# One change in three places of an attention and mixture-of-experts kernel: softmax scalings with an accumulator output, the second expert's rows transposed on TensorE, the last routing round's products placed later

## The chip, the cores and the metric

The kernel runs on one core of one Trainium2 chip. Its engines are TensorE (PE, with its weight loads counted apart as PEld), VectorE (DVE), ScalarE (ACT), GpSimd (POOL) and SyncE (SP), which here only issues DMAs. Each engine works through its own list of instructions in the order in which the program wrote them. The metric is the time of one execution on the device in microseconds, taken as the median of several runs.

## What is computed

Causal attention by blocks of 64 over 8 batches, 8 heads, 576 positions and a head size of 64; its output, as 4608 tokens of 512 numbers, goes through 8 experts. Each token is given to one expert, greedily by the largest logits, and each expert takes 576 tokens.

```python
scores = scale * np.matmul(q, k.transpose(0, 1, 3, 2))
scores = np.where(mask, scores, -1000000000.0)
scores = scores - np.max(scores, axis=-1, keepdims=True)
attn = np.exp(scores)
attn = attn / (np.sum(attn, axis=-1, keepdims=True) + 1e-09)
x = np.matmul(attn, v)          # then to (4608, 512)
logits = x @ w_gate             # (4608, 8)
for idx in np.argsort(-logits.flatten()):
    tok, e = idx // 8, idx % 8
    if assigned[tok] >= 0 or counts[e] >= 576: continue
    assigned[tok] = e; counts[e] += 1
for e in range(8):
    h = np.maximum(x[assigned == e] @ w1[e], 0.0)
    out[assigned == e] = h @ w2[e]
```

## The kernel before

**A planner writes the order.** All work is written as generators that yield steps such as `yield D, 70, events`: the engine (D is DVE, A is ACT, T is TensorE, G is POOL, S is SP), a planned cost in ns, and the planned events that the step needs. `Sched.run` (line 113) keeps a clock for each engine and always takes the step that could start first, with priorities for near ties. The order in which steps are taken is the order of the instructions on each engine. Planned costs and events set only that order; at run time an engine waits on semaphores for the data that an instruction really needs. A step that names two engines, 'AD' or 'GD', goes to the one whose planned end is earlier, with a bias.

**Attention** works on 32 pairs of heads (`n`), each as 128 partitions that hold a 64-row block of two heads. `scores` (line 330) multiplies with TensorE in three groups of row blocks, `GROUPS`; two score buffers exist in PSUM. `softmax` (line 355) runs once for each pair and group, 96 times: DVE takes row maxima (line 366), scales them by minus the softmax factor (line 369, two to four numbers per partition), ACT takes the exponential with these as bias and sums the rows (line 373), DVE adds 1e-9 to the sums (line 385) and takes the reciprocal (line 387), and POOL (line 395), in one case DVE (line 393), multiplies the probabilities. `transpose` (line 405) turns them with TensorE (line 421), and ACT (line 401) or DVE (line 403) copies them out of PSUM; the planner chooses. `values` (line 426) multiplies with v, `rows` writes x to DRAM, `logits` makes the logits. The small numbers of a pair stand in a tile `m` of [128, 4, 9]: row 0 maxima, row 1 scaled maxima, row 2 sums, row 3 reciprocals. DVE also makes a shifted copy of k (line 327) and residuals of q and k (line 277, DVE or POOL).

**Experts.** `route(k)` (line 653) finds in 14 search steps (lines 712 to 737: counts on DVE and ACT, a small TensorE product `tot`) the expert that fills up next and its threshold. It then numbers its tokens with the TensorE products `po` (lines 794 to 801) and DVE steps (803 to 814), updates the logits in `out` (lines 817 to 824, with `full`, lines 784 to 788) and so starts route k+1. `invert` (line 828) turns the numbers into a list of row indices: comparisons OH and OL and products RH on DVE (lines 832 to 839), TensorE products `pe` (line 846) and `ps` (line 853), the list `ix` at line 856. For k = 0 one of the RH products is ACT's (line 833) and `out` comes after the RH step, as `s.late`. The last round, k = 7, has no search.

`gather` (line 910) fetches the expert's rows with five indirect DMAs from POOL's queue. `flip` (line 923) brings them into column form: for k = 0 with eight TensorE transposes for each block of 128 rows (line 928) and a copy by ACT and one by DVE (lines 932, 933), for the others with a DMA transpose from SP's queue (line 942). `weights` (line 865) loads an expert's weights in eight pieces of 512 KB from SP's queue; ACT and POOL (for the first pieces of experts 0 and 1 ACT and DVE) split them into two half-precision parts (lines 876 to 889). The second four pieces of expert 1 wait in the plan for the event 'fl',1, that its rows have been flipped.

`ffn(k)` (line 945) makes h (line 967, in two halves of tokens), its halves HH and HL (lines 953, 955), then y for five blocks of rows (lines 992, 996). `yev` copies y out (line 975, for the last block also line 979) and scatters it to the output with an indirect DMA from POOL's queue (line 983); three output buffers `y` exist.

The lines that set the places spoken of:

```python
yield D,440 if k==0 else 800                       # 837
yield T,350,'rt'                                   # 841: before the pe products
yield G,1038,('ffn',k-2),('xm',k-1,m)              # 915: before a gather
yield G,1038,('yo',s.ny-1)                         # 982: before a scatter
```

## Time and profile before

| | |
|---|---|
| median of 3 runs | 846.4 us (844.75 to 847.79) |
| the profiled execution | 841.47 us, its span 839.7 us |
| granted TensorE clock, mean | 0.948 |
| PE busy | 736.4 us (88%) |
| DVE busy | 628.2 us (75%) |
| ACT busy | 533.3 us (64%) |
| POOL busy | 458.2 us (55%) |
| DMA traffic | 126.77 MB, 151 GB/s on average |

The profile is one execution, recorded by the hardware profiler. A group's row gives the line of the program, engine, operation, tiles (out<-in), shapes and count; behind the first bar the busy us of the group and the mean ns of one; behind the second the idle time of the engine just before them and what ended it. A row of the view of one line gives minimum, median and maximum ns. A row of the timeline gives the start in us, the duration in us and, in brackets, how long the engine had been idle and what released it. The chain of waits is followed back from the last instruction, at each step to what released it.

Attention ends at about 372 us. A routing round with TensorE mostly idle follows to about 412 us, then the eight experts to about 825 us, then the last scatters.

### The profile page before, as it was taken

The numbers are of one execution on the slowest core, as the hardware profiler recorded it, in microseconds if no ns is written. First come the engines' busy times: TensorE is split into PE (matmuls) and PEld (weight loads), VectorE is DVE, ScalarE is ACT, GpSimd is POOL, SyncE is SP. The second block draws the span as 40 slices with busy tenths as digits, with TensorE's granted clock in tenths as the row PEclk, the third lists the DMA queues.
The fourth block names the chain that finished last, engine by engine and source line by source line (L and its number), as shares of the span: only waits on it lengthen the run. The fifth ranks groups of instructions, "written<-read, shape, count | busy, mean of one in ns | idle before, by whom it ended". The sixth has DMA issues, their size and how long they took to land.

```text
span 839.7 us, 18356 instructions
## 1 busy us (share of the span) xinstructions
PE 736.4 (88%) x6253; PEld 460.4 (55%) x6253; DVE 628.2 (75%) x2300; ACT 533.3 (64%) x1443; POOL 458.2 (55%) x497
## 2 busy tenths in 40 slices
PE   5888998888898889971599699999999997999995
PEld 3555555555565566650454474756647464475752
DVE  7999999899989999748798796977778697020210
ACT  5777876677787777824483487777684947373210
POOL 5787776677776777610240346647390835665101
PEclk9999998899999999985699899999999999999998
DMA  9799998899879989732613718375563919763101
GB/s 193 146 184 165 189 182 160 161 185 203 188 143 175 180 162 200 171 77 57 214 45 121 201 51 269 103 247 118 206 150 118 232 45 277 220 137 76 33 13 44
DMA packets 291757, 126.77 MB, mean 151 GB/s; under 512 B 256336, under 2 KB 274768, under 8 KB 291664
## 3 DMA queue, kind: packets, MB, share of 16 engines
q1 hardware_dynamic: 285776, 106.73, 58.0%
q0 software_dynamic: 5888, 18.88, 7.4%
q8 instruction: 49, 0.80, 0.4%
q14 instruction: 44, 0.36, 0.1%
HBM read 71.32 MB, written 18.87 MB: 107 GB/s over the span
## 4 chain that ended last, share of the span: by engine, by line
PE 44%; DVE 16%; DMA 5%; issue 4%; ACT 3%; POOL 2%; SPq 0%; POOLq 0%; DVEq 0%; ACTq 0%
PE h L967 19%; PE y L992 15%; DVE m L366 3%; PE psb L421 3%; DMA raw<-in_moe_w_dram 2%; PE y L996 2%; PE psb L456 2%; ACT P L373 2%; DVE jk L719 1%; DMA xg<-x,ix 1%; DVE kS L327 1%; PE psb L348 1%; DVE PT L403 1%; DVE m L369 1%; DVE jk L720 1%
## 5 line engine op out<-in xcount | busy, mean ns | idle before, releaser
L395 POOL TENSOR_TENSOR P<-P,m 128x448 f32<-128x448 f32 (+8 forms) x287 | 214.3, 776 | 87.6 <-DVE m L387 44.7
L967 PE MATMUL h<-X,W 128*128 128x320 f16 (+3 forms) x1536 | 197.4, 288 | 3.3 <-DMA X<-xg 3.3
L373 ACT ACTIVATE P<-psb,m 128x576 f32<-128x576 f32 (+8 forms) x288 | 148.1, 529 | 70.2 <-DVE m L369 66.7
L967 PEld LDWEIGHTS <-W 128*128 128x128 f16 x1536 | 143.0, 99 | 46.2 <-DMA X<-xg 3.3
L992 PE MATMUL y<-W,HH 128*128 128x512 f16 x512 | 153.1, 381 | 0.0
L889 POOL TENSOR_TENSOR W<-raw,W 128x1024 f16<-128x1024 f32 x56 | 118.3, 2136 | 55.9 <-ACT W L887 55.5
L421 PE MATMUL psb<-mident,P 128*128 128x128 f32 (+1 forms) x800 | 117.0, 294 | 29.5 <-DVE XT L441 13.9
L366 DVE TENSOR_REDUCE m<-psb 128x1 f32<-128x576 f32 (+8 forms) x288 | 127.7, 478 | 8.2 <-PE psb L348 7.8
L421 PEld LDWEIGHTS psb<-mident,P 128*128 128x128 f32 (+1 forms) x800 | 93.7, 149 | 58.1 <-issue 24.4
L983 POOL DMA_INDIRECT out_dram<-yo,ix x40 | 39.0, 976 | 127.5 <-ACT yo L975 77.0
L456 PE MATMUL psb<-PT,vn 128*64 128x448 f32 (+6 forms) x784 | 107.6, 395 | 1.1 <-ACT P L373 0.7
L348 PE MATMUL psb<-kT,qT 128*64 128x512 f16 (+7 forms) x640 | 88.6, 301 | 12.0 <-ACT P L373 11.2
L992 PE MATMUL y<-W,HL 128*128 128x512 f16 x256 | 97.3, 380 | 0.0
L953 ACT ACTIVATE HH<-h 128x320 f16<-128x320 f32 (+3 forms) x128 | 52.1, 409 | 68.0 <-PE h L967 66.4
L348 PEld LDWEIGHTS <-qT 128*64 128x64 f16 x1280 | 62.0, 111 | 55.4 <-issue 40.0
L401 ACT ACTIVATE PT<-psb 128x512 f32<-128x512 f32 (+1 forms) x166 | 81.1, 546 | 15.9 <-PE psb L421 15.2
L955 DVE SCALAR_TENSOR_TENSOR HL<-h,HH 128x320 f16<-128x320 f32 (+3 forms) x128 | 56.9, 452 | 38.7 <-ACT HH L953 38.2
L348 PE MATMUL psb<-kS,qT 128*64 128x512 f16 (+7 forms) x640 | 84.4, 294 | 0.0
L918 POOL DMA_INDIRECT xg<-x,ix x40 | 39.6, 991 | 74.3 <-DVE ix L856 45.6
L992 PEld LDWEIGHTS <-HH 128*128 128x128 f16 x512 | 46.8, 98 | 52.0 <-issue 1.8
L975 ACT ACTIVATE yo<-y 128x512 f32<-128x512 f32 (+1 forms) x40 | 23.6, 591 | 72.4 <-PE y L992 63.0
L883 ACT ACTIVATE raw<-raw 128x512 f32<-128x512 f32 x112 | 67.4, 625 | 2.4 <-DMA raw<-in_moe_w_dram 2.3
(197 smaller groups left out, 1081.0 us busy)
## 6 DMA issues: line engine op xcount, KB each, us to landing
raw<-in_moe_w_dram SPq DMA_DIRECT2D x64, 512.0 KB, 5.1
x<-XR SPq DMA_DIRECT2D x16, 576.0 KB, 5.7
kn<-in_k_dram SPq DMA_DIRECT2D x15, 576.0 KB, 5.6
qn<-in_q_dram SPq DMA_DIRECT2D x15, 576.0 KB, 7.8
vn<-in_v_dram SPq DMA_DIRECT2D x64, 128.0 KB, 2.9
vn<-in_v_dram SPq DMA_DIRECT2D x16, 64.0 KB, 2.9
xg<-x,ix POOLq DMA_INDIRECT x40, 4.3
out_dram<-yo,ix POOLq DMA_INDIRECT x40, 2.8
```

What stands on the lines that cost most here:

```text
L348: nc.tensor.matmul(ps[64 * h:64 * h + 64, o + a:o + e], lhsT=A[:, h, 64 * i:64 * i + 64], rhs=K[:, h, a:e], start=st, stop=not st)
L366: nc.vector.tensor_reduce(m[:, 0, c:c + 1], ps[:, o:o + 64 * (i + 1)], axis=AX.X, op=OP.max)
L373: nc.scalar.activation(Pt[:, s.OFF[i]:s.OFF[i] + 64 * (i + 1)], ps[:, o:o + 64 * (i + 1)], AF.Exp, bias=m[:, 1, c:c + 1], scale=s.ESC, acc ...
L395: nc.gpsimd.tensor_tensor(sl, sl, m[:, 3, c:c + 1].to_broadcast([P, w]), op=OP.mult)
L401: s.nc.scalar.activation(out, in_, AF.Copy)
L421: nc.tensor.transpose(ps[0:w, a], s.Pb[n % s.NP][:, s.OFF[i] + 128 * j:s.OFF[i] + 128 * j + w], s.ident)
L456: nc.tensor.matmul(ps[64 * h:64 * h + 64, 64 * (i0 - b0):64 * (b1 - b0)], lhsT=vn[:kp, j, 2 * (n % 2) + h, :], rhs=pt[:kp, s.PTI[(j, i0)]: ...
L883: nc.scalar.activation(raw[:,x],raw[:,x],AF.Copy,scale=s.WS)
L889: nc.gpsimd.tensor_tensor(lw,raw,hi,op=OP.subtract)
L955: nc.vector.scalar_tensor_tensor(HL[:,f,ts],ps,0.0,HH[:,f,ts],op0=OP.max,op1=OP.subtract)
L967: nc.tensor.matmul(ps,lhsT=W[:,a,d,f*P:f*P+P],rhs=X[:,4*(d//2)+d%2+l,ts],start=(d==0 and n==0),stop=(d==3 and n==2))
L992: if m<4: nc.tensor.matmul(ps,lhsT=Z[:,f,m*P:m*P+P],rhs=Y[:,a,f],start=(f==n==0),stop=(f==7 and n==2))
```

## The change

It has three places.

1. The tile `m` gets a tenth column. Lines 369 and 385 get a second operation, an addition of 0, and an accumulator output into that column, which nobody reads. Their planned cost becomes 150 instead of 70.
2. The second expert (k = 1) is treated as the first was: its rows are transposed by TensorE and copied by ACT and DVE instead of by DMA transposes; one RH product goes to ACT; `out` of route 1 comes after the RH step (`full` stays where it was). The scatters of the first expert's blocks 2 to 4 wait in the plan until the second expert's gathers have been issued.
3. For the last round a planned event 'hold' sets the `po` products and the `pe` products each 8 us later in the plan. For the other rounds the event is due at once.

```diff
--- before.py
+++ after.py
@@ -356,7 +356,7 @@
         nc, sc = s.nc, s.sc
         G = s.GROUPS[g]
         if g == 0:
-            s.d['m', n] = s.wp.tile([P, 4, 9], F32, tag="m", name=f"m{n}", bufs=4)
+            s.d['m', n] = s.wp.tile([P, 4, 10], F32, tag="m", name=f"m{n}", bufs=4)
         m, Pt = s.d['m', n], s.Pb[n % s.NP]
         c0 = s.COL[G[0][0]]
         c1 = c0 + len(G)
@@ -365,8 +365,9 @@
             yield D, 65 + 1.042 * 64 * (i + 1)
             nc.vector.tensor_reduce(m[:, 0, c:c + 1], ps[:, o:o + 64 * (i + 1)], axis=AX.X, op=OP.max)
             sc.nolat()
-        yield D, 70
-        nc.vector.tensor_scalar(m[:, 1, c0:c1], m[:, 0, c0:c1], -s.ESC, None, op0=OP.mult)
+        yield D, 150
+
+        nc.vector.tensor_scalar(m[:, 1, c0:c1], m[:, 0, c0:c1], -s.ESC, 0.0, op0=OP.mult, op1=OP.add, accum_out=m[:, 0, 9:10])
         for i, o in G:
             c = s.COL[i]
             yield A, 237 + .835 * 64 * (i + 1), ('ptd', n - s.NP)
@@ -381,8 +382,8 @@
         if g == 2:
             G = [x for y in s.GROUPS[s.RM:] for x in y]
             c0, c1 = s.COL[G[0][0]], 9
-        yield D, 70, *[('e', n, x) for x in range(s.RM if g == 2 else g, g + 1)]
-        nc.vector.tensor_scalar(m[:, 3, c0:c1], m[:, 2, c0:c1], 1e-9, None, op0=OP.add)
+        yield D, 150, *[('e', n, x) for x in range(s.RM if g == 2 else g, g + 1)]
+        nc.vector.tensor_scalar(m[:, 3, c0:c1], m[:, 2, c0:c1], 1e-9, 0.0, op0=OP.add, op1=OP.add, accum_out=m[:, 2, 9:10])
         yield D, 88
         nc.vector.reciprocal(m[:, 3, c0:c1], m[:, 3, c0:c1])
         for i, _ in G:
@@ -787,7 +788,8 @@
             V.tensor_tensor(Lm,Lm,be(u),op=OP.add)
             sc.busy(D,520)
         if not last and k: full()
-        yield T,80,'rt'
+        s.hold(k)
+        yield T,80,'rt',('hold',k)

         tk=sc.take(); ps=s.ps.tile([P,512],F32,tag="rt",name=f"po{k}")
         pos=ps[:,:2*C].rearrange("p (i c) -> p i c",i=2)
@@ -822,23 +824,27 @@
                 V.tensor_tensor(Lm,Lm,b3(q[:,3]),op=OP.subtract)
                 sc.set(('Lm',k+1))
                 sc.add(s.route(k+1),0,sc.now)
-            if k: sc.add(out(),0,sc.now)
+            if k>1: sc.add(out(),0,sc.now)
             else: s.late=out
         yield from s.invert(k,L16,h2)
+    def hold(s,k):
+
+        s.sc.ev['hold',k]=s.sc.now+(8000 if k==s.E-1 else 0)
     def invert(s,k,L16,h2):
         nc=s.nc; rp=s.rp; C=s.C; V=nc.vector; sc=s.sc
         yield D,440
         OH=rp.tile([P,20,C],F16,tag="OH",name=f"OH{k}"); RH=rp.tile([P,2,20,C],F16,tag="RH",name=f"RH{k}")
         V.tensor_tensor(OH,s.io5,h2[:,None,:].to_broadcast([P,20,C]),op=OP.is_equal)
-        if k==0: nc.scalar.activation(RH[:,1],OH,AF.Copy,scale=s.pc)
+        if k<2: nc.scalar.activation(RH[:,1],OH,AF.Copy,scale=s.pc)
         yield D,700
         OL=rp.tile([P,32,C],F16,tag="OL",name=f"OL{k}",bufs=1)
         V.tensor_tensor(OL,s.iom,L16[:,None,:].to_broadcast([P,32,C]),op=OP.is_equal)
-        yield D,440 if k==0 else 800
+        yield D,440 if k<2 else 800
         V.tensor_tensor(RH[:,0],OH,s.tok,op=OP.mult)
-        if k: V.tensor_scalar(RH[:,1],OH,s.pc,None,op0=OP.mult)
+        if k>1: V.tensor_scalar(RH[:,1],OH,s.pc,None,op0=OP.mult)
         else: sc.add(s.late(),0,sc.now)
-        yield T,350,'rt'
+        s.hold(k)
+        yield T,350,'rt',('hold',k)
         tk=sc.take(); ps=s.ps.tile([P,512],F32,tag="rt",name=f"pe{k}")

         for c in range(C):
@@ -922,19 +928,20 @@
             sc.add(s.flip(k,m,n,xg,X),1,sc.now)
     def flip(s,k,m,n,xg,X):
         nc=s.nc; sc=s.sc
-        if k==0:
+        if k<2:
             yield T,8*107,('xg',k,m),('xm',k,m-2)
-            ps=s.ps.tile([P,8,P],F16,tag="xt",name=f"xt{m}",bufs=2)
+            ps=s.ps.tile([P,8,P],F16,tag="xt",name=f"xt{k}_{m}",bufs=2)
             for j in range(8): nc.tensor.transpose(ps[:,j,:n],xg[:n,P*j:P*j+P],s.idh[:n,:n])
             def ev(j):
                 yield (A,480) if j else (D,600)
                 o,i=X[:,4*j:4*j+4,m*P:m*P+n],ps[:,4*j:4*j+4,:n]
                 if j: nc.scalar.activation(o,i,AF.Copy)
                 else: nc.vector.tensor_copy(o,i)
-                s.half[m]=s.half.get(m,0)+1
-                if s.half[m]==2: sc.set(('xm',k,m))
+                s.half[k,m]=s.half.get((k,m),0)+1
+                if s.half[k,m]==2: sc.set(('xm',k,m))
             for j in range(2): sc.add(ev(j),0,sc.now)
-            if m<s.NWM:
+            if m==4: sc.set(('fl',k))
+            if k==0 and m<s.NWM:
                 for _ in range(2): nc.tensor.matmul(s.wu,lhsT=s.ones,rhs=xg[:,:512],start=True,stop=True)
                 sc.busy(T,430)
             return
@@ -979,7 +986,7 @@
                 nc.vector.scalar_tensor_tensor(y[:n],ps[:n],sca,y[:n],op0=OP.mult,op1=OP.add)
             sc.set(gk)

-            yield G,1038,('yo',s.ny-1)
+            yield G,1038,('yo',s.ny-1),('gi',1) if k==0 and m>1 else None
             nc.gpsimd.indirect_dma_start(out=s.out,out_offset=bass.IndirectOffsetOnAxis(ap=s.ix[k][:n,m:m+1],axis=0),in_=y[:n],in_offset=None)

             sc.soft(728,('yo',s.ny)); sc.ev['yo',s.ny]=max(sc.ev['yo',s.ny],sc.now+4500); s.ny+=1
```

## The prediction

> **What bounds the kernel now.** I read the table of windows first, since the program has stages with different limits: attention up to about 372 us, routing of the first expert to about 412, then eight rounds of expert products. Behind the stretch and its length stand busy us and instructions of PE, its weight loads, DVE, ACT and POOL, then granted clock, DMA share and GB/s.
>
> ```profile
> 0.00:358.00 358.00, 309.51 (x3013) 201.68 (x3015) 329.28 (x841) 267.53 (x821) 258.55 (x356) 0.96 0.91 176
> 222.00:372.00 150.00, 136.64 (x1392) 90.54 (x1388) 126.55 (x334) 110.20 (x341) 97.92 (x126) 0.98 0.83 165
> 462.00:476.00 14.00, 7.63 (x51) 3.36 (x49) 11.87 (x55) 6.54 (x15) 7.32 (x7) 0.87 0.72 175
> 709.00:718.00 9.00, 3.63 (x52) 1.44 (x50) 6.12 (x8) 2.34 (x5) 3.63 (x2) 0.82 1.03 287
> 760.00:823.00 63.00, 63.00 (x391) 36.52 (x391) 8.51 (x18) 13.53 (x29) 11.44 (x10) 1.00 0.10 31
> ```
>
> Attention: DVE is busy 329.3 of 358 us (92%), PE 309.5 (86%). No engine is full; DVE is nearest. Among the experts PE is full (63 of 63 in the last long window) with two holes, at 462 to 476 and 709 to 718. The change touches attention's DVE and both holes. Next, what DVE's busy time consists of: the views of single source lines (minimum/median/maximum in ns), the chain of waits for 222 to 372 us (it has nothing before 217), and who waits.
>
> ```profile
> L369 DVE TENSOR_SCALAR m<-m x96: 155/325/1318, 13.2 to 352.8; 128x2 f32<-128x2 f32 x32, 128x3 f32<-128x3 f32 x32, 128x4 f32<-128x4 f32 x32
> L385 DVE TENSOR_SCALAR m<-m x96: 138/169/1202, 15.8 to 355.2; 128x2 f32<-128x2 f32 x32, 128x3 f32<-128x3 f32 x32, 128x4 f32<-128x4 f32 x32
> L720 DVE TENSOR_SCALAR_CACHE_REDUCE jk<-m_P,cd x84: 499/508/514, 434.3 to 686.1; 128x288 f16<-128x288 f32 x84
> L720 DVE DVE_READ_ACCUMULATOR jk<-m_P,cd x84: 80/85/89, 434.8 to 686.5; 128x1 f16 x84
> L672 DVE TENSOR_SCALAR_CACHE_REDUCE MM<-m_vm x1: 191/191/191, 704.9 to 704.9; 128x36 f16<-128x36 f32 x1
> L327 DVE COPY kS<-kT x32: 453/511/1397, 8.6 to 325.4; 64x1152 f16<-64x1152 f16 x32
> ```
>
> ```profile
> L369 DVE TENSOR_SCALAR m<-m 128x2 f32<-128x2 f32 (+2 forms) x96 | 45.1, 470 | 2.5
> L385 DVE TENSOR_SCALAR m<-m 128x2 f32<-128x2 f32 (+2 forms) x96 | 29.6, 308 | 7.0 <-ACT P L373 6.4
> L401 ACT ACTIVATE PT<-psb 128x512 f32<-128x512 f32 (+1 forms) x166 | 81.1, 546 | 15.9 <-PE psb L421 15.2 <-ACT PT L401 0.2
> L403 DVE COPY PT<-psb 128x512 f32<-128x512 f32 (+1 forms) x58 | 36.6, 652 | 2.7 <-PE psb L421 2.6
> ```
>
> ```profile
> by line: PE psb L421 17.5%; DVE m L366 16.0%; PE psb L456 10.9%; ACT P L373 10.6%; issue 6.6%; DVE kS L327 5.4%; PE psb L348 5.1%; DVE m L369 4.8%; DVE PT L403 4.3%; DVE m L385 3.9%; DVE XT L441 3.0%; POOL P L395 2.1%; DVE XT L439 1.9%; DVE
> ```
>
> ```profile
> ACT P L373 <- DVE m L369: 66.7, 53, 3.7
> ```
>
> Two to four numbers per partition cannot cost 1.3 us of arithmetic. The plain scalings of lines 369 and 385 are held up by something, and the form with an accumulator is not: line 720, 84 times beside POOL's weight work, stays within 499 to 514 ns.
>
> **Part A, the accumulator on lines 369 and 385.** Removed: 45.1 + 29.6 = 74.7 us of DVE time. Added: 192 instructions of the other form. The trace lacks them at 2 to 4 elements; line 672's 191 ns at 36 elements is above them and line 369's 155 ns minimum is about their floor, so I take 158, near the floor, because line 672 carries 32 more elements. Each brings a read of 85 ns: 192 x 0.243 = 46.7 us. DVE loses 74.7 - 46.7 = 28 us of busy time. The read need not cost its full length:
>
> ```profile
> 462.91 0.51 DVE L720 TENSOR_SCALAR_CACHE_REDUCE jk<-m_PB,bs 128x288 f16<-128x288 f32 x1
> 463.35 0.09 DVE L720 DVE_READ_ACCUMULATOR jk<-m_PB,bs 128x1 f16 x1
> 463.35 0.51 DVE L720 TENSOR_SCALAR_CACHE_REDUCE jk<-m_PB,bs 128x288 f16<-128x288 f32 x1
> ```
>
> Here the next operation starts together with the read, 0.44 us after one of 0.51. So 28 us is a cautious figure for DVE; with the read hidden it is 44. The Trainium skill says, in VectorE: DVE Perf Modes, section The DRAIN you can't avoid, that the next operation waits until the pipeline is empty, which would make the added reads cost their whole 192 x 0.085 = 16.3 us; that gives the 28, and these rows disagree with it.
>
> What of the 28 us shortens the stage? The chain gives lines 369 and 385 4.8% and 3.9% of 150 us: 7.2 and 5.9 us. The part of them that goes is (470 - 243)/470 = 48% and (308 - 243)/308 = 21%: 3.5 + 1.2 = 4.7 us in 150, so 11 us in 358. Ends: 0 if the next engine was as late everywhere, 28 if DVE set every step. I take 14, near the chain's 11, a little above because ACT's 66.7 us of waiting for line 369 and POOL's and PE's waits behind it shrink too. PE is late next: its 309.5 us are a floor 48 us away. The planned costs of both steps rise from 70 to 150 ns, 15.4 us over the stage, so the written order shifts everywhere in attention; no row prices that, and it is why I keep both ends.
>
> **Part B, the second expert's rows.** Rows of the hole:
>
> ```profile
> 455.82 0.19 DVE L820 TENSOR_TENSOR q<-q,MM 128x36 f32<-128x36 f32 x1
> 456.64 0.53 DVE L832 TENSOR_TENSOR OH<-m_io,h 128x720 f16<-128x720 f16 x1
> 461.33 0.17 DVE L856 CAST ix<-ps 128x5 int32<-128x5 f32 x1 [0.73 <-PE ps L853]
> 463.00 0.96 POOL L983 DMA_INDIRECT out_dram<-yo,ix  x1 [6.93 <-ACT m_PB L688]
> 464.26 1.59 POOL L918 DMA_INDIRECT xg<-x,ix  x1 [0.30 <-issue]
> 468.70 0.38 PE L996 MATMUL y<-W,HL 128*64 128x512 f16 x2
> 475.80 3.38 PE L967 MATMUL h<-X,W 128*128 128x256 f16 x15 [3.26 <-DMA X<-xg]
> 479.25 0.16 DVE L737 SCALAR_TENSOR_TENSOR sg<-tot,m_wk 128x3 f32<-128x3 f32 x1 [4.95 <-PE tot L734]
> 481.15 2.12 PE L967 MATMUL h<-X,W 128*128 128x256 f16 x18
> ```
>
> ```profile
> DMA to landing us min/median/max: 3.5/4.3/8.3
> ```
>
> ```profile
> 412.64 1.28 PE L928 MATMUL xt<-m_idh,xg 128*128 128x128 f16 x16 [2.27 <-DMA xg<-x,ix]
> 418.07 0.41 PE L928 MATMUL xt<-m_idh,xg 64*128 64x64 f16 x8
> ```
>
> The indices are ready at 461.50; a scatter at 463.00 goes first on POOL, so the first gather starts at 464.26. With three scatters placed behind the gathers it starts 0.3 us after the indices, 2.5 us earlier, and 0.8 more because line 820's three steps no longer stand ahead of line 832. The gather moves to about 461.0 and its landing (median 4.3) to 465.3, while PE still has expert 0's products until 469.08. The five DMA transposes go. PE now stands still from 469.08 to 475.80, 6.7 us, and then runs 15 products in 3.38 us where 18 take 2.12: 1.6 us more. Added on PE: 40 transposes at the rate of 1.28 us per 16 and 0.41 for the last 8: 3.0 us. The ten copies lie on ACT and DVE beside them; without that cover each is about 0.5 us, once. Sum: 6.7 + 1.6 - 3.0 = 5.3 us. The scatters wait longer; nobody reads them before the end, and three output buffers cover the delay. Line 833's product with the partition number goes to ACT. SP's wait for the flips before the second half of expert 1's weights falls earlier too.
>
> Late next is expert 2's first weights:
>
> ```profile
> 521.29 6.32 POOL L889 TENSOR_TENSOR W<-raw,W 128x1024 f16<-128x1024 f32 x3
> 528.55 2.31 PE h L967 x21
> ```
>
> They end at 527.6, 0.9 us before use. They follow route 2, which itself lost 4.95 us to PE's standstill (the row at 479.25); that comes back, so they move about 5 us too. I take 5 of the 5.3. Ends: 1 if gathers land after 8.3 us (4 more, which PE would wait out in its order), 6.
>
> **Part C, the last round.**
>
> ```profile
> 706.34 6.29 POOL L889 TENSOR_TENSOR W<-raw,W 128x1024 f16<-128x1024 f32 x3
> 706.53 6.15 DVE L812 TENSOR_SCALAR h<-q 128x36 f16<-128x36 f32 x1
> 714.84 0.91 PE L846 MATMUL pe<-RH,OL 128*32 128x40 f16 x36 [5.37 <-DVE RH L839]
> 715.69 1.04 PE L992 MATMUL y<-W,HH 128*128 128x512 f16 x2
> 718.37 0.60 PE L992 MATMUL y<-W,HH 128*128 128x512 f16 x2
> 733.35 0.98 POOL L918 DMA_INDIRECT xg<-x,ix  x1 [0.30 <-DMA raw<-in_moe_w_dram]
> ```
>
> Line 812 lasts as long as POOL's three operations; lines 814 to 839 follow it, and the products of line 846 stand in PE's order ahead of ready expert work. PE loses 5.37 us and then runs slowly until 718.37 (1.04 against 0.60 twice: 0.9). The hold sets line 794 and line 846 each 8 us later in the order, so PE has work while DVE waits. Even if line 812 meets such a burst again, 6.15 us and the following steps (712.7 to 714.8, 2.1) make 8.3, against 8 plus the planned time of those steps. The gathers of the last expert start at 733.35 today and its rows are used only at 783, so 16 us of delay less the stall is covered. Behind it PE is full to 823, so the gain stays: 6 us, ends 4 and 6.3.
>
> **Sum.** 14 + 5 + 6 = 25 us. The profiled execution took 841.5 us (span 839.7 and 1.8 around it), so it would be 816.5. The median of the three runs is 4.9 above that execution; I take the 25 from the median: 821 us.
>
> **Rivals.** (1) DVE sets all of attention: 28 instead of 14, so 807. For it: 92% busy, and the hidden reads. Against: eight other lines share the chain. (2) The waiting moves. Line 327's copy ranges from 453 to 1397 ns, so it is held up as well; what lines 369 and 385 give up may be waited out there, or PE's order may be as late anyway. A is 0 and the time 846 - 11 = 835. The Trainium skill states such a rule in SBUF — State Buffer, section Who interferes with whom: copies, scalings without an accumulator output, and operations with two SBUF inputs share a port pair with POOL, the later one blocked for the whole instruction; line 327 is such a copy. (3) Gathers land late, B is 1: 825. (4) Slower: the planner, believing DVE dearer, hands line 403's copies to ACT, 0.546 us each. If ACT's 66.7 us of waiting do not shrink, each lengthens the stage; all 58 add 31.7 us, so 846 - 11 + 32 = 867. It turns slower from 21 of them (11.5 us). Against: ACT at 267.5 us has 42 us less work than PE, and DVE sheds 36.6 us. That the new form does not escape the hold-up, line 720 speaks against.
>
> **How the numbers follow.** Forecast 0.50; (1) 0.18; (2) 0.16; (3) 0.08; (4) 0.08. The range 804 to 839 holds the first four with their bounds (846 - 28 - 6 - 6.3 = 806 and 2 us of hidden reads at the fast end, A 0 and B 1 at the slow end) and leaves out (4) and the tails. About 0.3%, 2.5 us, is what a measurement here can tell from no change. Faster by more: the first four less 0.02 for the upper tail of (2): 0.90. Same: that tail and the lowest start of (4), 0.03. Slower: 0.07.
>
> **What would show it.** Lines 369 and 385 become a main part of under 200 ns with no long maximum, and a read of 85; ACT's wait for line 369 falls well below 66.7 us; the logits end near 358 instead of 372. No transposes by DMA for the second expert, PE's hole at 469 gone, line 846 of the last round without a wait. The forecast is wrong if line 327 or line 277 grows by as much as the scalings shrink, if ACT becomes the fullest engine of attention, or if expert 2's products wait for weights.

## The result

The changed kernel took 810.3 us (median of 4 runs, 808.9 to 815.8) where the kernel before took 846.4 (844.8 to 847.8): a ratio of 0.959, 95% interval 0.954 to 0.964, 36 us less. The forecast was 821 with a range of 804 to 839. The profiled execution took 811.16 us, its span 809.4, with a granted clock of 0.960.

The sum was 11 us short, and its parts fell out otherwise than the total suggests. First the ends of the stages, from the timeline of PE of the kernel before: attention's last product with v, the first product of the first expert, the last of the last one.

```profile
370.93 0.81 PE L456 MATMUL psb<-PT,vn 128*64 128x192 f32 x8
...
415.20 1.81 PE L967 MATMUL h<-X,W 128*128 128x128 f16 x15
...
829.98 0.38 PE L992 MATMUL y<-W,HL 128*128 128x512 f16 x1
```

The same three places in the kernel after, whose line numbers are 1 higher in attention and 7 among the experts:

```profile
338.13 0.81 PE L457 MATMUL psb<-PT,vn 128*64 128x192 f32 x8
...
382.59 1.11 PE L974 MATMUL h<-X,W 128*128 128x128 f16 x15
...
799.34 0.38 PE L999 MATMUL y<-W,HL 128*128 128x512 f16 x1
```

Attention is 32.8 us shorter (370.93 - 338.13), where the forecast had 14. From the first to the last product of the experts it is 416.8 us against 414.8: in these two executions the eight experts won nothing, where the forecast had 11. Attention's lines first, by the views of single lines (minimum/median/maximum ns) and the list of waits (us in total, times, longest):

```profile
L370 DVE TENSOR_SCALAR_CACHE_REDUCE m<-m x96: 150/156/159, 12.8 to 320.0; 128x2 f32<-128x2 f32 x32, 128x3 f32<-128x3 f32 x32, 128x4 f32<-128x4 f32 x32
L370 DVE DVE_READ_ACCUMULATOR m<-m x96: 81/83/85, 12.9 to 320.1; 128x1 f32 x96
...
L386 DVE TENSOR_SCALAR_CACHE_REDUCE m<-m x96: 136/147/158, 15.7 to 322.3; 128x2 f32<-128x2 f32 x32, 128x3 f32<-128x3 f32 x32, 128x4 f32<-128x4 f32 x32
L386 DVE DVE_READ_ACCUMULATOR m<-m x96: 74/83/85, 15.8 to 322.4; 128x1 f32 x96
```

```profile
ACT P L374 <- DVE m L370: 28.1, 28, 3.2
```

The long maxima of 1318 and 1202 ns are gone, the durations taken for the new form (158 ns; medians 156 and 147) and for its read (85; 83) were close, and ACT's wait for this line fell from 66.7 to 28.1 us. What held the plain scalings up can be read from the trace of the kernel before: all 52 of line 369 that lasted more than 215 ns, and all 36 of line 385 that lasted more than 200, started beside a running instruction of POOL and ended 22 to 29 ns behind its end. The 29 shorter ones that started beside POOL did so in the last 190 ns of its instruction. Of the new form 75 and 66 of 96 start beside POOL in the run a_form below, up to 1.2 us ahead of its end, and none lasts more than 159 ns.

Two groups of DVE in the kernel after show what else moved: the copies of line 403 (404 now) stay on DVE, 57 of 58, and of the subtractions of line 277 on k eight have gone from DVE (23 before, 15 now) to POOL.

```profile
L404 DVE COPY PT<-psb 128x512 f32<-128x512 f32 (+1 forms) x57 | 35.4, 647 | 5.1 <-PE psb L422 4.2 <-ACT PT L402 0.5 <-ACT P L374 0.2
L277 DVE TENSOR_TENSOR k<-kn,k 128x576 f16<-128x576 f32 x15 | 16.9, 1129 | 0.2 <-ACT k L270 0.2
```

Now the two holes among the experts, in the timeline. The eight weight loads of the second expert, issued from SP's queue between 420.72 and 431.12, its first gather, and the first transposition of its rows:

```profile
420.72 10.40 SPq L910 DMA_DIRECT2D raw<-in_moe_w_dram  x8
427.02 1.00 POOL L924 DMA_INDIRECT xg<-x,ix  x1 [4.42 <-DVE ix L862]
433.87 0.62 PE L934 MATMUL xt<-m_idh,xg 128*128 128x128 f16 x8 [1.86 <-DMA xg<-x,ix]
```

The first gather starts 44.4 us behind the first expert's first product (427.02 - 382.59) instead of 49.1 (464.26 - 415.20), but its rows are in use only 6.85 us later, and PE waits for them. The last round:

```profile
685.78 6.39 DVE L814 TENSOR_SCALAR h<-q 128x36 f16<-128x36 f32 x1
692.21 0.20 DVE L816 SCALAR_TENSOR_TENSOR L<-q,h 128x36 f16<-128x36 f32 x1
692.32 0.54 DVE L837 TENSOR_TENSOR OH<-m_io,h 128x720 f16<-128x720 f16 x1
692.78 5.39 DVE L841 TENSOR_TENSOR OL<-m_iom,L 128x1152 f16<-128x1152 f16 x1
698.54 0.40 DVE L844 TENSOR_SCALAR RH<-OH,m_pc 128x720 f16<-128x720 f16 x1
698.99 0.92 PE L852 MATMUL pe<-RH,OL 128*32 128x40 f16 x36 [2.50 <-DVE RH L844]
```

Line 814 meets POOL's weight work again (three products, 6.29 us from 685.84), as reckoned; then line 841 meets the next burst (two products, 4.21 us from 693.34), and PE waits 2.50 us instead of 5.37. And there is a stall that no step spoke of, in the search of the fourth expert's threshold: the product of line 735 is recorded at 575.34, DVE gets its sum only at 578.04, and the next product of this kind comes after 2.15 us in which PE stands still.

```profile
575.34 0.17 PE L735 MATMUL tot<-cn,m_bo 128*128 128x3 f16 x1
...
578.04 0.16 DVE L738 SCALAR_TENSOR_TENSOR sg<-tot,m_wk 128x3 f32<-128x3 f32 x1 [3.47 <-PE y L999]
...
579.63 0.18 PE L735 MATMUL tot<-cn,m_bo 128*128 128x3 f16 x1 [2.15 <-ACT yo L982]
```

Two questions follow: why a DVE microsecond was worth so much more in attention than reckoned, and whether the second and third edit were really worth nothing.

### The profile page after: what moved, and what is told of

Same layout as the page of the kernel before. It is cut to its first block, busy times and chain, and to the rows that moved or that the text cites. A ratio compares the mean times of both kernels' runs of the same rounds, so it can differ in the third digit from the quotient of the medians.

```text
span 809.4 us, 18606 instructions
## 1 busy us (share of the span) xinstructions
PE 724.1 (89%) x6293; PEld 449.3 (56%) x6293; DVE 588.9 (73%) x2489; ACT 536.5 (66%) x1447; POOL 466.9 (58%) x506
## 4 chain that ended last, share of the span: by engine, by line
PE 60%; DVE 19%; ACT 7%; DMA 6%; issue 4%; POOL 2%; another core or an unknown queue 0%; POOLq 0%; SPq 0%; DVEq 0%; ACTq 0%
PE h L974 22%; PE y L999 14%; PE psb L422 8%; PE psb L457 6%; DVE m L366 5%; PE psb L348 5%; DMA kT<-k 3%; PE y L1003 2%; DVE kS L327 2%; ACT W L893 2%; POOL P L396 2%; DMA xg<-x,ix 1%; DVE jk L720 1%; ACT P L374 1%; ACT raw L889 1%
## 5 line engine op out<-in xcount | busy, mean ns | idle before, releaser
L396 POOL TENSOR_TENSOR P<-P,m 128x576 f32<-128x576 f32 (+8 forms) x288 | 211.4, 765 | 52.9 <-DVE m L388 19.5
L974 PE MATMUL h<-X,W 128*128 128x320 f16 (+3 forms) x1536 | 195.1, 286 | 0.5 <-issue 0.4
L374 ACT ACTIVATE P<-psb,m 128x576 f32<-128x576 f32 (+8 forms) x288 | 148.2, 535 | 32.2 <-DVE m L370 28.1
L422 PE MATMUL psb<-mident,P 128*128 128x128 f32 (+1 forms) x800 | 109.1, 281 | 17.1 <-POOL P L396 5.8
L422 PEld LDWEIGHTS psb<-mident,P 128*128 128x128 f32 (+1 forms) x800 | 86.5, 141 | 47.4 <-POOL P L396 19.2
L402 ACT ACTIVATE PT<-psb 128x512 f32<-128x512 f32 (+1 forms) x167 | 82.8, 553 | 21.2 <-PE psb L422 18.5
L348 PE MATMUL psb<-kT,qT 128*64 128x512 f16 (+7 forms) x640 | 86.6, 298 | 6.8 <-ACT P L374 4.5
L348 PEld LDWEIGHTS <-qT 128*64 128x64 f16 x1280 | 59.4, 111 | 48.0 <-issue 32.0
L348 PE MATMUL psb<-kS,qT 128*64 128x512 f16 (+7 forms) x640 | 80.7, 291 | 0.4 <-DVE kS L327 0.4
L893 ACT ACTIVATE W<-raw 128x512 f16<-128x512 f32 x112 | 68.9, 631 | 0.0
```

The source lines that it names most:

```text
L348: nc.tensor.matmul(ps[64 * h:64 * h + 64, o + a:o + e], lhsT=A[:, h, 64 * i:64 * i + 64], rhs=K[:, h, a:e], start=st, stop=not st)
L374: nc.scalar.activation(Pt[:, s.OFF[i]:s.OFF[i] + 64 * (i + 1)], ps[:, o:o + 64 * (i + 1)], AF.Exp, bias=m[:, 1, c:c + 1], scale=s.ESC, acc ...
L396: nc.gpsimd.tensor_tensor(sl, sl, m[:, 3, c:c + 1].to_broadcast([P, w]), op=OP.mult)
L402: s.nc.scalar.activation(out, in_, AF.Copy)
L422: nc.tensor.transpose(ps[0:w, a], s.Pb[n % s.NP][:, s.OFF[i] + 128 * j:s.OFF[i] + 128 * j + w], s.ident)
L893: nc.scalar.activation(hi[:,x],raw[:,x],AF.Copy)
```

## Experiments on attention

The first four kernels shared a chip on which the kernel before took 845.9 us (median of 13 runs).

**a_form**: the accumulator alone, with the order of every engine unchanged.

```
-  nc.vector.tensor_scalar(m[:, 1, c0:c1], m[:, 0, c0:c1], -s.ESC, None, op0=OP.mult)
+  nc.vector.tensor_scalar(m[:, 1, c0:c1], m[:, 0, c0:c1], -s.ESC, 0.0, op0=OP.mult, op1=OP.add, accum_out=m[:, 0, 9:10])
...
   (line 385 likewise; the planned costs stay 70)
```

> The kernel before with the accumulator output on lines 369 and 385 alone; planned costs stay at 70, so that every engine gets the same instructions in the same order as before. Theory F (the form): a plain scaling waits for POOL's hold on the shared access, the accumulator form does not, and the whole 33 us by which attention became shorter come from that: about 813 us, first expert product at about 382 us, line 369 at 150 to 160 ns with a read of 80 to 85, line 366's waits and ACT's waits for line 369 at 28 us or so. Rival O (the order): much of the 33 came from the planner, which now believes these steps dearer and places them otherwise: 826 us or above. Rival S (the shares of the prediction: 14 us for the accumulator, 11 for the rest): 832.

**a_order**: the planned costs alone.

```
-  yield D, 70
+  yield D, 150
...
   (line 384 likewise; the scalings stay plain)
```

> The kernel before with only the planned costs of the steps of lines 369 and 385 raised from 70 to 150; the scalings keep their plain form. Theory F: the order by itself is worth nothing or costs a little, 844 to 852 us. Rival O: 833 us or less, as the planner then sees DVE's load more nearly as it is (line 369's mean of 470 ns and line 385's of 308).

**a_only**: both of these on the kernel before, nothing among the experts.

> The accumulator and its planned costs on the kernel before, without the two changes among the experts. Theory F: 811 to 814 us, all of the 36 us that the change brought or nearly so, first expert product at about 382 us; the time from there to the last y product 410 us as before (409.8), against 411.8 with the whole change. Rival S: 832 us, with 11 us of the gain missing.

Measured: a_form 817.6 us, ratio 0.966 (0.962 to 0.970); a_order 847.5, 1.001 (0.998 to 1.003); a_only 814.1, 0.961 (0.957 to 0.965). The form by itself is worth 29 us (theory F had 33), the dearer planned costs by themselves nothing. Rivals O and S (826 and 832) fall. Whether both together are worth 4 us more than the form (0.961 against 0.966) stays open, since the intervals overlap. The expectations of a_only and bc_only count the experts to the first product of the last block (825.01 and 794.36), which gives their 409.8 and 411.8 us where the whole is 414.8 and 416.8.

a_form is the clean case, since only DVE's instructions change. The table of windows for the whole of attention, first the kernel before, then a_form (busy us of PE, its loads, DVE, ACT, POOL, then granted clock, DMA share and GB/s):

```profile
0.00:371.74 371.74, 323.25 (x3179) 210.74 (x3180) 334.70 (x857) 271.68 (x828) 258.74 (x356) 0.96 0.88 171
```

```profile
0.00:337.47 337.47, 306.78 (x3179) 198.78 (x3180) 300.19 (x1049) 268.83 (x828) 259.35 (x356) 0.99 0.99 188
```

DVE is busy 34.5 us less and the stage is 34.3 us shorter; DVE's share is 90% before and 89% after. Most of the 34.5 can be traced: the scalings fall from 74.7 to 29.2 us (96 x 0.156 + 96 x 0.148), 45.5 less, and their 192 reads lie beside other work: with the rows of the reads left out, DVE's busy time is only 0.4 us lower. Of the 45.5 line 277 takes back 7 us, as its group on k shows, before and then in a_form. That is a small piece of rival 2, the waiting that moves. Small growth of other lines takes back 2 us, and overlaps of neighbouring rows make up the 2 that remain.

```profile
L277 DVE TENSOR_TENSOR k<-kn,k 128x576 f16<-128x576 f32 x23 | 18.8, 816 | 0.0
...
L277 DVE TENSOR_TENSOR k<-kn,k 128x576 f16<-128x576 f32 x23 | 25.7, 1119 | 0.0
```

PE's busy time falls too, by 16 us for the same 3179 products, at a granted clock of 0.99 instead of 0.96; a_369 and a_twice below show that the clock is not what shortens the stage. By the time of the whole kernel a_form is worth 29 us and not 34: among the experts its profile takes 421.4 us, 6.6 more than that of the kernel before, but a_order's on the same chip takes 422.0, so this is not the form's.

The kernel after has another order, in which DVE does eight of these subtractions less:

```profile
0.00:338.94 338.94, 307.84 (x3179) 198.62 (x3180) 290.13 (x1042) 271.46 (x826) 265.73 (x365) 0.98 0.97 187
```

DVE is down to 290.1 us there, 86% of the stage, and the stage is no shorter than a_form's. PE has 307.8 us, 91%: the one for one of DVE ends about here.

**a_369**: the form on line 369 alone, line 385 plain, same order.

> The accumulator form on line 369 alone, at the old planned costs and the same order; line 385 stays plain. Line 369 gives back 45.1 - 96 x 0.156 = 30 us of DVE time, line 385 would 29.6 - 96 x 0.147 = 15.5 more. Theory D: two thirds of the 28 us that both brought, so 826 to 828 us, line 385 plain and still with a long maximum. Rival E (only line 369 stands on ACT's way to the exponentials, line 385's sums are waited for by POOL, which has slack): 817 to 820, line 385 worth nothing.

**a_twice**: a_form with each scaling issued twice.

```
-  nc.vector.tensor_scalar(..., accum_out=m[:, 0, 9:10])
+  nc.vector.tensor_scalar(..., accum_out=m[:, 0, 9:10]); nc.vector.tensor_scalar(..., accum_out=m[:, 0, 9:10])
...
   (line 385 likewise)
```

> The kernel with the accumulator form at the old planned costs, and each of the 192 scalings issued twice in succession, the second with the same operands and result. Every other engine gets the same instructions in the same order. The second one costs DVE about its main part, 0.15 us, its read lying beside the first one's or the next operation: 192 x 0.15 = 29 us more of DVE time. Theory D (DVE sets attention almost everywhere, so that a microsecond of DVE is about 0.8 of the stage, as 34 us for 43 were): 23 us more, 840 us. Rival C (the share of the chain of waits in the prediction, 11 of 28 us): 11 us more, 829. Rival W (not DVE's time counted but its longest holds of up to 1.3 us, which stood in ACT's way): 5 us more or less, 820 to 823.

Both on a chip where the kernel before took 842.3 us: a_369 824.7, ratio 0.979 (0.975 to 0.984); a_twice 839.7, 0.996 (0.994 to 0.999). Against a_form on the other chip, issuing twice costs 0.996 - 0.966 of 842, 25 us; theory D had 23, C 11, W 5. And line 369 alone brings 17 of the 29 us, line 385 the rest, near the two thirds of DVE's time: rival E falls. The windows of attention, a_369 and then a_twice:

```profile
0.00:352.10 352.10, 312.29 (x3179) 203.47 (x3180) 317.31 (x953) 270.42 (x828) 259.89 (x356) 0.98 0.93 180
```

```profile
0.00:367.09 367.09, 315.81 (x3179) 205.05 (x3180) 331.05 (x1433) 271.02 (x828) 257.94 (x356) 0.98 0.89 173
```

Two neighbouring scalings in a_twice's timeline, and the operation behind them:

```profile
100.35 0.14 DVE L385 TENSOR_SCALAR_CACHE_REDUCE m<-m 128x4 f32<-128x4 f32 x1
100.42 0.08 DVE L385 DVE_READ_ACCUMULATOR m<-m 128x1 f32 x1
100.53 0.16 DVE L385 TENSOR_SCALAR_CACHE_REDUCE m<-m 128x4 f32<-128x4 f32 x1
100.62 0.08 DVE L385 DVE_READ_ACCUMULATOR m<-m 128x1 f32 x1
100.62 0.62 DVE L366 TENSOR_REDUCE m<-psb 128x1 f32<-128x448 f32 x1
```

In the windows DVE has 30.9 us more than in a_form and the stage is 29.6 us longer. Four kernels with one order of work (before, a_form, a_369, a_twice) lie near one line, with DVE at 89 to 90% of the stage each time: a microsecond of DVE's busy time is about a microsecond of attention. a_369 and a_twice settle the clock: both have 0.98, PE is busy 312 and 316 us, and with 13.7 us more of DVE the stage is 15.0 us longer.

The added operation is the one at 100.53, 0.18 us behind its twin and behind the twin's read (in the median 0.19 us on line 385 and 0.20 on line 369). So the 192 added take about 37 us of DVE's queue, though 30.9 of its busy time, and the stage shows 0.8 of that. An operation of another line does not wait for the read: line 366 starts together with it at 100.62, and in a_form the next operation starts 70 to 74 ns ahead of the end of the main part in the median, where it was 85 behind the plain form. The prediction had taken from the Trainium skill (VectorE: DVE Perf Modes, The DRAIN you can't avoid) that the next operation waits for an empty pipeline; the same paragraph adds that a next operation that is not held starts earlier, and the operations behind these reads do.

## Experiments among the experts

**bc_only**: the whole change without the accumulator and its costs, on the first chip.

```
-  ... -s.ESC, 0.0, op0=OP.mult, op1=OP.add, accum_out=m[:, 0, 9:10])
+  ... -s.ESC, None, op0=OP.mult)
...
   (line 385 likewise; planned costs back at 70)
```

> The two changes among the experts without the accumulator. If they are worth what the prediction said (5 and 6 us): 835 us. If they give back later what they win, as the profile of the whole change suggests (first h to last y 411.8 us against 409.8): 844 to 848 us, with first h at 415 us, h of the third expert 2.6 us earlier relative to it, and the gain gone by the last y.

Measured: 837.1 us, ratio 0.988 (0.984 to 0.992), 9 to 10 us less than the kernel before. The second expectation, that the gain is given back, falls; without the accumulator the two parts bring what the prediction had for them (11). The next four shared a chip on which the kernel before took 841.5 us.

**after2**: the changed kernel unaltered.

> The changed kernel once more, unaltered, to set the next three beside it on one chip: ratio to the kernel before near 0.959. Theory L (the place, not luck): its profile again has the late search product of the fourth round, about 195 us after the first expert's first product, with DVE waiting 2 to 3 us for it. Rival N (such stalls fall anywhere and by chance): none there this time, or another place.

**no_b**: it without the second expert's part.

```
-  if k>1: sc.add(out(),0,sc.now)
+  if k: sc.add(out(),0,sc.now)
...
-  if k<2:
+  if k==0:
...
-  yield G,1038,('yo',s.ny-1),('gi',1) if k==0 and m>1 else None
+  yield G,1038,('yo',s.ny-1),None
```

> The changed kernel without the second expert's part (accumulator and last round's hold stay): the rows go by DMA transposes again, three scatters ahead of the gathers. Theory L: the second expert wins 6 us at the third expert's first product and loses 4 again at the stall near 195 us, which belongs to its order; net 2, so 812 where the changed kernel has 810, and no stall at 195. Prediction's step B: 5 us more than the changed kernel. Rival: nothing, the same time within 1 us.

**no_c**: it without the hold of the last round.

```
-  s.sc.ev['hold',k]=s.sc.now+(8000 if k==s.E-1 else 0)
+  s.sc.ev['hold',k]=s.sc.now+0
```

> The changed kernel with the last round's hold at 0 instead of 8000. Theory L: TensorE's wait before the last round's products goes from 2.5 us back to 5.4 and its slow stretch with it: 3 us more than the changed kernel. Prediction's step C: 6 us more. Rival: the same time, the wait only moves to another place.

Measured, 6 runs each: after2 803.8 us, ratio 0.958 (0.953 to 0.962); no_b 805.3, 0.958 (0.954 to 0.961); no_c 811.3, 0.964 (0.961 to 0.966). The profile of after2, the same program as the kernel after, at three places: its first expert product, the search product where the other execution stalled (192.7 us behind the first product in both), and its last product.

```profile
383.08 1.79 PE L974 MATMUL h<-X,W 128*128 128x128 f16 x15
...
575.76 0.17 PE L735 MATMUL tot<-cn,m_bo 128*128 128x3 f16 x1
576.00 0.16 DVE L738 SCALAR_TENSOR_TENSOR sg<-tot,m_wk 128x3 f32<-128x3 f32 x1 [0.31 <-PE tot L735]
...
790.15 0.38 PE L999 MATMUL y<-W,HL 128*128 128x512 f16 x1
```

No stall: rival N was right, and theory L wrong. The experts take 407.1 us in this execution and 416.8 in the other, of one and the same program; the kernel before took 414.8 in its profiled execution, and a_form, with the same order of work, 421.4. So single profiles of this kernel differ among the experts by nearly 10 us, and the "nothing won" read from two of them is no measure of the change. Sums as late as that (1.5 to 4.8 us from the product of line 734 to line 737, where 0.2 to 1.1 is usual) stand in five profiles, all four of the first chip and that of the kernel after, in two places each or more, and in none of the nine others. They are not all of the spread: a_twice has none and takes 421.7 us, and of the 9.7 us between the two executions 6.2 lie between the third expert's first h product and the sixth's first y product, where two of its three late sums stand, and 2.7 in the last round. What makes them isn't settled; the edits don't, as a_form and a_order have the experts' code of before.

The hold: PE's wait ahead of the last round's products in no_c, then in after2.

```profile
680.74 0.91 PE L852 MATMUL pe<-RH,OL 128*32 128x40 f16 x36 [5.38 <-DVE RH L844]
```

```profile
692.41 0.91 PE L852 MATMUL pe<-RH,OL 128*32 128x40 f16 x36 [1.36 <-DVE RH L844]
```

From the sixth expert's first y product to the seventh's first h product no_c takes 32.0 us and after2 26.2, as their windows show:

```profile
670.59:702.62 32.03, 26.65 (x169) 11.72 (x166) 9.89 (x16) 12.88 (x25) 24.00 (x16) 0.89 0.86 224
```

```profile
670.10:696.25 26.15, 24.79 (x170) 11.41 (x167) 13.64 (x16) 12.88 (x25) 22.16 (x14) 1.00 0.97 262
```

That is 5.9 us, part C's 6: 4.0 of waiting (5.38 - 1.36) and 1.9 of PE's busy time, whose granted clock is 1.00 instead of 0.89. By the ratios it is 5, by the medians 7.5, and the intervals of the two ratios just touch. In all seven profiles without the hold that stretch takes 31.4 to 32.3 us; with it 26.0 to 26.2 in bc_only, after2 and no_b, and 28.9 in the kernel after. The second burst meets line 841 in all four (4.9 to 5.4 us). What sets the kernel after apart is that line 814 waited longer too (6.39 us against 5.3): PE waited 2.50 us instead of 1.1 to 1.4 and was then busy 26.4 us at a clock of 0.94.

Part B: from the first expert's first product to the third's it is 110.0, 110.2, 110.5 and 110.9 us in after, after2, bc_only and no_c, which have the part, and 112.5 to 116.6 in the seven that have not (mean 114.9). The three other runs that have it, brake, no_add and no_add_h below, take 112.1, 112.3 and 113.8, so the two groups are not clean apart. On one chip, and with no late sum in the stretch, no_b takes 114.6 against 110.2 and 110.9: about 4 us at that place, a little under the predicted 5. In the time no_b and after2 are not apart (medians 1.6 us, ratios 0), so how much of it reaches the end is not settled.

**brake**: the second half of expert 1's weight loads kept behind the gathers.

```
-  elif k>0: yield S,25,'hw',('wc',k-1,n+2),('fl',1) if k==1 and n>=4 else None
+  elif k==1 and n==4:
+      yield G,60,('gi',1),('wc',k-1,n+2)
+      raw=wp.tile([P,1024],F32,tag="raw",name=f"raw{k}_{wd}_{d}",bufs=6)
+      nc.gpsimd.memset(raw[:,0:1],0.0)
+      yield S,25,'hw'
...
+  elif k>0: yield S,25,'hw',('wc',k-1,n+2),('gi',1) if k==1 and n>=4 else None
```

> The changed kernel with one wait added: the loads of the second expert's other four weight blocks are issued behind a small GpSimd memset that stands behind the five gathers, so that they no longer share the DMA engines with them. If those loads stretched the gathers (6.85 us to the first landing against 3.96 before the change), the landing is back near 4 us, TensorE's 2.9 us of waiting for the rows go, and the kernel is 2 to 4 us faster than the changed kernel. Rival: the weights come later instead and the second expert's second products wait for them: no change or some us slower.

Measured: 806.7 us, ratio 0.960 (0.956 to 0.964), not faster than the changed kernel (after2, 803.8). Its timeline:

```profile
428.25 0.99 POOL L929 DMA_INDIRECT xg<-x,ix  x1 [4.40 <-DVE ix L862]
...
433.09 0.61 PE L939 MATMUL xt<-m_idh,xg 128*128 128x128 f16 x8
...
440.00 0.63 ACT L889 ACTIVATE raw<-raw 128x512 f32<-128x512 f32 x1 [2.95 <-DMA raw<-in_moe_w_dram]
...
442.51 0.16 PE L735 MATMUL tot<-cn,m_bo 128*128 128x3 f16 x1 [2.86 <-ACT ja L694]
```

The rows are now in use 4.84 us behind the first gather instead of 6.85, and PE does not wait for them; by the records of landings the first gather takes 3.9 us here (428.25 to 432.17) and 6.7 in after2 (428.07 to 434.75). The loads did stretch the gathers. But ACT then waits 2.95 us for weights, its count of the search comes late, and PE waits 2.86 us for that: the wait changes its place, as the rival had it.

## Two attempts to go further

On the last chip the kernel before took 841.8 us.

**no_add**: the changed kernel without the addition of 1e-9 (the sum is at least 1).

```
-  yield D, 150, *[('e', n, x) for x in range(s.RM if g == 2 else g, g + 1)]
-  nc.vector.tensor_scalar(m[:, 3, c0:c1], m[:, 2, c0:c1], 1e-9, 0.0, op0=OP.add, op1=OP.add, accum_out=m[:, 2, 9:10])
-  yield D, 88
-  nc.vector.reciprocal(m[:, 3, c0:c1], m[:, 3, c0:c1])
+  yield D, 88, *[('e', n, x) for x in range(s.RM if g == 2 else g, g + 1)]
+  nc.vector.reciprocal(m[:, 3, c0:c1], m[:, 2, c0:c1])
```

> The changed kernel without the addition of line 385: the reciprocal is taken of the sum itself (the sum holds the exponential of the largest score, 1, so that in 32 bits 1e-9 more is the same number). DVE loses 96 x 0.147 = 14 us in attention. Theory D (DVE still sets attention, one microsecond for one): the stage 10 to 14 us shorter than the changed kernel's, ratio to the kernel before near 0.942, 792 us where the changed kernel has 804. Rival P (DVE is level with TensorE and ACT by now, and they are late next): 5 us or less, ratio 0.952 or above.

**no_add_h**: that, and line 814 as two operations of the accumulator form.

```
-  V.tensor_scalar(h2,sl,1.5*2.0**28,1.5*2.0**28,op0=OP.add,op1=OP.subtract)
+  hb=rp.tile([P,C+1],F32,tag="hb",name=f"hb{k}")
+  V.tensor_scalar(hb[:,:C],sl,1.5*2.0**28,0.0,op0=OP.add,op1=OP.add,accum_out=hb[:,C:])
+  V.tensor_scalar(h2,hb[:,:C],-1.5*2.0**28,0.0,op0=OP.add,op1=OP.add,accum_out=hb[:,C:])
```

> The kernel without the addition, and the experts' rounding on line 814 written as two operations of the accumulator form, which are not held up by GpSimd's weight work. If that hold (5.3 to 6.4 us in the last round) is what still makes TensorE wait ahead of the last round's products (1.4 to 2.5 us and its slow stretch), these go: 2 to 3 us faster than without it. Rival: line 841, a comparison of two operands from SBUF, is held up by the same burst, so nothing changes; within 1 us.

no_add took 808.8 us, ratio 0.961 (0.958 to 0.964): no faster against its kernel before than the changed kernel (0.958), and its attention ended at 344.8 us where after2's did at 340.1. Theory D foretold 10 to 14 us less. The groups of DVE for after2, then no_add:

```profile
L404 DVE COPY PT<-psb 128x512 f32<-128x512 f32 (+1 forms) x57 | 35.5, 647 | 6.3 <-PE psb L422 5.5 <-ACT PT L402 0.5
L277 DVE TENSOR_TENSOR k<-kn,k 128x576 f16<-128x576 f32 x15 | 16.5, 1099 | 0.2 <-ACT k L270 0.2
...
L277 DVE TENSOR_TENSOR q<-qn,q 128x576 f16<-128x576 f32 x10 | 9.8, 983 | 0.8 <-ACT q L270 0.8
```

```profile
L402 DVE COPY PT<-psb 128x512 f32<-128x512 f32 (+1 forms) x66 | 41.5, 657 | 5.9 <-PE psb L420 5.3 <-ACT P L374 0.4
L277 DVE TENSOR_TENSOR k<-kn,k 128x576 f16<-128x576 f32 x18 | 20.2, 1121 | 0.6 <-ACT k L270 0.6
L277 DVE TENSOR_TENSOR q<-qn,q 128x576 f16<-128x576 f32 x15 | 16.3, 1088 | 0.2 <-ACT q L270 0.2
```

The planner, which now believes DVE lighter, gave it nine more copies and eight more subtractions: 41.5 - 35.5 + 20.2 - 16.5 + 16.3 - 9.8 = 16 us, more than the 14.3 that were taken away. So DVE got no lighter, and the run can't tell D from P, though P's number came out. Whether the removal pays with the old distribution wasn't tried.

no_add_h took 824.7 us, ratio 0.978 (0.975 to 0.981), 16 us more than no_add. Its last round:

```profile
708.87 0.19 DVE L814 TENSOR_SCALAR_CACHE_REDUCE h<-hb 128x36 f16<-128x36 f32 x1
...
709.11 3.94 DVE L816 SCALAR_TENSOR_TENSOR L<-q,h 128x36 f16<-128x36 f32 x1
...
714.08 4.93 DVE L843 TENSOR_TENSOR RH<-OH,m_tok 128x720 f16<-128x720 f16 x1
```

The new form of line 814 is not held up, but the next operation with two operands from SBUF is, 3.94 us where 0.20 is its time, and line 843 after it, 4.93 where 0.52 is; POOL works on weights from 706.68 to 712.98 and from 714.39 to 718.60. This is the rule in the Trainium skill, SBUF — State Buffer, section Who interferes with whom, once more: the accumulator form passes POOL's lock, an operation with two SBUF inputs waits for it. In the last round PE no longer waits; the loss lies elsewhere: the third expert's first products, in the timeline of PE, wait for weights. From its first product to the fourth expert's it is 62.3 us, where no_add takes 50.1.

```profile
512.85 1.03 PE L974 MATMUL h<-X,W 128*128 128x256 f16 x4 [4.58 <-POOL W L895]
```

The step's planned cost rose from 88 to 300 ns as well, and it runs in every round; which of the two disturbed the rounds was not taken apart. Neither attempt beats the changed kernel.

## Why the prediction came out as it did

**What bounds the kernel**: right. DVE was the nearest to full in attention, and the scalings were held up by something that the accumulator form escapes: POOL's instructions, by their ends in the trace.

**Part A, DVE's time**: 28 us by the cautious figure, 44 with the reads hidden. Measured 45.5 for the scalings themselves, of which line 277 takes back 7 and overlaps and other lines 4; 34.5 net. The reads are hidden; the rows of line 720, in which the next operation starts together with the read, were the ones to follow.

**Part A, what of it shortens the stage**: this is the step that went wrong. "I take 14, near the chain's 11", half of DVE's 28, where the runs show nearly all of it: 34.3 of 34.5 us in a_form, 29.6 of 30.9 in a_twice. The share that a line has in the chain of waits says how often that line stood on one path; it left out that every later DVE step starts earlier when any DVE step before it in the queue gets shorter, which is how I explain the one for one (argued; what is shown is the ratio). Rival 1, DVE sets all of attention, is what happened, and it was given 0.18; its price of 28 was too small for the same reason as above. The objection raised against it, eight other lines on the chain, was none: the quoted row names ten, and five of them are DVE's as well (366, 327, 403, 441 and 439, 30.6% together).

**Part A, the planned costs**: worth nothing alone. The planner moved eight subtractions to POOL; line 403's copies stayed, so rival 4 did not come about, though no_add shows the planner doing its mirror image.

**Part B**: 5 forecast, about 4 at the third expert in the profiles of one chip, unresolved in the time. Against the very profile that the working was made from, 112.5 us, the kernel after gains 2.5. Its lower end named gathers that land late, and they did: in use 6.85 us after issue instead of the 4.3 assumed. In the kernel before SP issued the second four loads at 478.09, behind its transposes; without these all eight go out from 420.72. PE then waits 2.7 us for rows (1.86 in the row shown and two shorter waits), a term that the forecast had at nothing: 5.3 - 2.7 = 2.6 is near the 2.5 measured.

**Part C**: 6 forecast, 5.9 in after2 against no_c. The working's terms were 5.4 of waiting and 0.9 of slow products; measured were 4.0 and 1.9, since line 841 met a second burst of POOL's work, which the working had not placed, while the products, at a granted clock of 1.00 instead of 0.89, gained more than reckoned. Between the profile before and that of the kernel after it was 2.5 (31.4 to 28.9).

**The sum**: 25 forecast, 36 measured. The parts measured one by one give 29 to 33 (A), about 4 (B) and 5 to 6 (C), 38 to 43, a little more than the whole; without the accumulator B and C bring 10 us, with it (0.961 to 0.958) about 3, on different chips and with intervals of 3 to 4 us. Whether they really hinder each other stays open. That the time fell inside 804 to 839 is partly luck: A's 33 us and the 10 that B and C bring without it would have made 803.

## What to carry to other kernels

Where an engine that works in order is 90% busy over a whole stage, reckon that an edit to it may count nearly one for one, as it did here until PE was at 91%, even if the chain of waits gives the single line less, and test that by issuing the operation twice. Look for short operations whose maximum is many times their minimum: compare their ends with the ends of other engines' instructions. Another form of the same operation may pass what holds them up; then see which operation is held up in its place. Where a planner deals out the work, the planned cost is part of the edit: an engine that is made lighter in the plan is filled up again.

## What the hardware showed that was not expected

The read of an accumulator costs DVE next to nothing where another line's operation follows: 192 of them, 15.8 us by their rows, add 0.4 us to DVE's busy time in a_form. A second scaling of the same numbers does wait for it, 0.19 to 0.20 us from start to start. A plain scaling of two to four numbers that starts beside a running instruction of POOL, more than 190 ns ahead of its end, lasts until 22 to 29 ns behind that end. Eight weight loads issued around a gather (DMA share 1.04, 401 GB/s from 427 to 434 us, the row below from the kernel after) stretched it from 3.9 us (464.26 to 468.20 before) to 6.85 until its rows were in use.

```profile
427.00:434.00 7.00, 5.14 (x29) 2.37 (x27) 6.37 (x24) 5.02 (x9) 5.76 (x5) 1.00 1.04 401
```

And one program's executions can differ by 10 us in 810, 6.2 of them in a stretch with two sums of a small product that reach DVE late. Such sums, 1.5 to 4.8 us late, stand in all four profiles of one chip and in that of the kernel after, and in none on three other chips. Why is open.
